# A build-time scheduler's three limits, constant before, now taken from a table by stretch of the run

## The chip, the cores and the metric

The kernel runs on one core of a Trainium2 chip. The metric is the device time of one execution in microseconds, median over several executions. "PE" in profile lines is TensorE's matmul, "PEld" its weight load, "DVE" is VectorE, "ACT" ScalarE, "POOL" GpSimd, "SP" the queue that issues most DMAs. All executions used here were in the fast state. One execution of each kernel was profiled; it can lie up to two microseconds from that kernel's median, so accounts inside an execution are made from profiles, and verdicts from medians and intervals.

## The reference, cut to what matters

A transformer block on 2048 tokens of width 512, with 32 heads of width 16 and a gated feed-forward part of width 1792.

```python
scores = jnp.einsum('bhqd,bhkd->bhqk', q, k) * Dh ** (-0.5)
p = _softmax(scores, axis=-1)
o = jnp.einsum('bhqk,bhkd->bhqd', p, v)
...                                   # output projection, residual, layer norm with modulation
return _gelu(x @ w_gate) * (x @ w_up) @ w_down
```

What costs is the exp: 32 x 2048 x 2048 scores, which the kernel handles as 2048 **blocks** of 128 x 512 scores of one head: 128 partitions, 512 columns.

## The kernel before

The program is written out by Python code that runs when the kernel is built. It keeps a time model of each engine, and at every step decides which instruction comes next. The chip then runs five fixed instruction streams. No scheduling happens on the chip.

ScalarE does most exps, three blocks in one instruction (a "triple") or two (a "pair"). VectorE takes some blocks by an integer trick, four at a time; these four are a **quad**. A quad also needs three shifted copies, each one instruction on VectorE or on GpSimd, and the values are then multiplied with all four copies.

```python
gb = self.scp[:, s0 + CH - 1, :]      # third bank of the group of three ...
if g is not None:                     # ... goes to VectorE when a quad is open
    ...
self.act(self.E[:, e0:e0 + n, :], self.scp[:, s0:s0 + n, :], ACT.Exp, scale=EXP_SCALE)
...
self.ts("dve", kq[:, 512 * j:512 * j + 512].bitcast(U16), gb, 128 / OCT, SHIFT_C, ALU.mult, ALU.add)
```

So an open quad turns ScalarE's triples into pairs. When a quad may open, and who does its shifts, depends on three limits:

```python
AHEAD = 20        # a round may become a quad only if it lies this many blocks ahead
PRESS = 5         # no exp to VectorE while a unit with so few plain rounds left lacks shifts
URGENT = 6        # a shift of a unit with so few plain rounds left goes first, and not to GpSimd
...
def urgency(self, tk):
    ...
    return 0 if self.plain[tk[1][1]] <= (URGENT if tk[1][1][3] == 512 else URG2) else 2
...
def pressed(self):
    return any(x.get("done", 0) < 3 and self.plain[x["rnd"][0]] <= (PRESS if x["rnd"][0][3] == 512 else PRE2) for x in self.wait)
```

A **unit** is one group of heads with one set of queries, a **round** is four blocks of a unit, and a quad is a round. The queries come in sets of 512, 512, 512, 256, 128 and 128 tokens, so attention has a long stage of 512-wide units and, from about 614 us, one of 256-wide units and then the last blocks. The feed-forward matmuls of a finished set are "side work", put into TensorE's gaps in the attention of the next sets. What is not done when attention ends is done in the **tail**, before the last 128 tokens can finish.

The time model gives a DMA a fixed time to land, which one of the experiments below changes:

```python
self.dma_free = max(t + 1400, self.dma_free) + cost / (350 if early else RATE)
op.t1 = self.dma_free + (1500 if early else LAND)          # LAND = 1300 ns
```

## Time and profile before

| | before |
|---|---|
| time, median of 4 | 807.35 us |
| profiled span | 805.0 us |
| ScalarE busy | 773.7 us (96%) |
| VectorE / TensorE / GpSimd busy | 83% / 93% / 34% |
| blocks on VectorE | 420 of 2048 (105 quads) |
| attention ends, tail | 778.0 us, then 27.0 us |

The table is read from top to bottom: ScalarE sets the time, VectorE's blocks relieve it, and the tail is what comes after the last exp of attention. The prediction shows the lines. Two lines that it uses without showing them are the groups by form of GpSimd's shifts in the kernel before (count, busy us, mean ns, then idle time before them and what ended it):

```profile
L393 POOL TENSOR_SCALAR mreg<-dreg 128x2048 uint16<-128x2048 uint16 x93 | 175.3, 1902 | 260.7 <-DVE mreg L393 105.7 <-PE ps_pv L368 41.2 <-DVE wreg L385 31.1
L393 POOL TENSOR_SCALAR mreg<-mreg 128x2048 uint16<-128x2048 uint16 x46 | 86.7, 1902 | 138.8 <-DVE mreg L393 47.1 <-DVE wreg L402 36.0 <-PE ps_pv L368 24.0
```

GpSimd does 93 + 46 = 139 of the 315 shifts.

### The profile page before, as it was taken

Reading aid. Unit: us, or ns where it says so; the run is one execution under the profiler, and the core shown is the slowest. Engines: PE = TensorE matmul, PEld = TensorE weight load, DVE = VectorE, ACT = ScalarE, POOL = GpSimd, SP = SyncE. Lnnn points to the kernel's source line nnn. Section 1 sums busy time; section 2 is a strip of 40 time slices with the busy share of each in tenths; the row PEclk is TensorE's granted clock in tenths of the full one; section 3 lists DMA queues with packets and bytes.
Section 4 is the critical chain, followed back from the end, with each engine's and each line's share of the span. In section 5 each row is a group of like instructions: output and inputs, shape, how many; then the busy total and the mean of one; then the engine's idle time right before and its main releaser. Section 6 shows DMA issues by size and latency. Waiting matters only on the chain.

```text
span 805.0 us, 27412 instructions
## 1 busy us (share of the span) xinstructions
PE 749.6 (93%) x12250; PEld 267.6 (33%) x12254; DVE 671.0 (83%) x1216; ACT 773.7 (96%) x728; POOL 277.7 (34%) x172
## 2 busy tenths in 40 slices
PE   8899999998899999999999899999999899999987
PEld 3333333322222222222222222222344342454455
DVE  7878898978898989988688998989778986677873
ACT  5999999999999999999999999999999999999982
POOL 3110335365546172456556346134262010000310
PEclk9999999999999999999999999999999999999999
DMA  9101000000022121111003111110123221120100
GB/s 310 58 9 19 10 10 16 10 16 10 16 55 68 35 55 36 48 41 29 24 27 108 36 52 51 48 42 17 42 59 89 63 75 37 34 75 14 23 9 14
DMA packets 58632, 36.03 MB, mean 45 GB/s; under 512 B 17977, under 2 KB 55090, under 8 KB 58514
## 3 DMA queue, kind: packets, MB, share of 16 engines
q1 hardware_dynamic: 56914, 32.84, 15.0%
q8 instruction: 96, 1.57, 0.8%
q10 hardware_dynamic: 1600, 1.44, 0.6%
q14 instruction: 22, 0.18, 0.1%
HBM read 29.62 MB, written 2.61 MB: 40 GB/s over the span
## 4 chain that ended last, share of the span: by engine, by line
ACT 89%; PE 8%; DVE 3%; issue 0%; DVEq 0%
ACT E L381 85%; PE ps_sc L368 4%; ACT wreg L381 3%; PE ps_mi L368 3%; PE ps_pv L368 1%; DVE mreg L393 1%; DVE kmo L402 0%; DVE xs L385 0%; DVE wreg L385 0%; PE ps_sc L372 0%; DVE hreg L393 0%; ACT L381 0%; DVE vaug L402 0%; DVE dreg L393 0%; DVE kme L393 0%
## 5 line engine op out<-in xcount | busy, mean ns | idle before, releaser
L381 ACT ACTIVATE E<-ps_sc 128x1024 bf16<-128x1024 f32 (+2 forms) x686 | 748.2, 1282 | 15.6 <-PE ps_sc L368 15.0
L393 POOL TENSOR_SCALAR mreg<-dreg 128x2048 uint16<-128x2048 uint16 x93 | 175.3, 1902 | 260.7 <-DVE mreg L393 105.7
L393 DVE TENSOR_SCALAR dreg<-ps_sc 128x512 uint16<-128x512 f32 x253 | 171.6, 685 | 34.3 <-PE ps_sc L368 31.8
L368 PE MATMUL ps_sc<-qT,kme 32*128 32x512 bf16 (+2 forms) x1313 | 168.3, 332 | 18.3 <-ACT E L381 15.1
L368 PE MATMUL ps_sc<-qT,kmo 32*128 32x512 bf16 (+2 forms) x1313 | 173.7, 332 | 9.7 <-ACT E L381 8.5
L368 PE MATMUL ps_pv<-E,vaug 128*17 128x512 bf16 (+2 forms) x2112 | 150.4, 327 | 0.8 <-DVE osb L402 0.5
L393 POOL TENSOR_SCALAR mreg<-mreg 128x2048 uint16<-128x2048 uint16 x46 | 86.7, 1902 | 138.8 <-DVE mreg L393 47.1
L368 PE MATMUL ps_pv<-mreg,vaug 128*17 128x512 bf16 (+2 forms) x1704 | 121.6, 337 | 1.7 <-DVE mreg L393 1.0
L393 DVE TENSOR_SCALAR mreg<-ps_sc 128x512 uint16<-128x512 f32 x126 | 85.4, 686 | 18.9 <-PE ps_sc L368 17.5
L368 PE MATMUL ps_mi<-wreg,mreg 128*32 128x512 bf16 (+1 forms) x1280 | 92.4, 372 | 4.4 <-DVE wreg L398 1.3
L368 PEld LDWEIGHTS ps_sc<-qT,kme 32*128 32x128 bf16 x1313 | 45.0, 91 | 143.7 <-ACT E L381 115.4
L368 PEld LDWEIGHTS ps_sc<-qT,kmo 32*128 32x128 bf16 x1313 | 45.7, 91 | 127.8 <-ACT E L381 109.3
L393 DVE TENSOR_SCALAR mreg<-dreg 128x2048 uint16<-128x2048 uint16 x117 | 76.8, 682 | 1.7 <-PE ps_pv L368 1.4
L368 PEld LDWEIGHTS ps_pv<-E,vaug 128*17 128x17 bf16 x2112 | 43.9, 89 | 61.5 <-issue 48.8
L368 PEld LDWEIGHTS ps_pv<-mreg,vaug 128*17 128x17 bf16 x1704 | 38.1, 89 | 36.8 <-issue 13.2
L402 DVE CAST wreg<-ps_mi 128x512 bf16<-128x512 f32 x49 | 33.5, 684 | 10.5 <-PE ps_mi L368 10.3
L368 PEld LDWEIGHTS ps_mi<-wreg,mreg 128*32 128x32 bf16 x1280 | 26.7, 95 | 44.0 <-issue 18.8
L368 PE MATMUL ps_mi<-hreg,wreg 128*32 128x512 bf16 x480 | 39.5, 385 | 0.0
L393 DVE TENSOR_SCALAR mreg<-mreg 128x2048 uint16<-128x2048 uint16 x59 | 38.4, 682 | 1.1 <-PE ps_pv L368 1.0
L398 DVE SCALAR_TENSOR_TENSOR wreg<-wreg,ps_mi 128x512 bf16<-128x512 bf16 x49 | 33.4, 682 | 6.5 <-PE ps_mi L368 5.1
L635 POOL TENSOR_SCALAR mv<-mv 128x4 f32<-128x4 f32 (+2 forms) x11 | 2.6, 239 | 94.5 <-DVE mv L425 93.9
L385 DVE TENSOR_TENSOR wreg<-wreg 128x1024 bf16<-128x1024 bf16 (+1 forms) x56 | 34.1, 616 | 0.5
(149 smaller groups left out, 670.8 us busy)
## 6 DMA issues: line engine op xcount, KB each, us to landing
mreg<-in_B_w_up_dram SPq DMA_DIRECT2D x22, 256.0 KB, 2.9
mreg<-in_B_w_gate_dram SPq DMA_DIRECT2D x15, 256.0 KB, 3.0
rb<-scr_rec SPq DMA_DIRECT2D x96, 32.0 KB, 1.8
dreg<-in_B_w_down_dram SPq DMA_DIRECT2D x9, 256.0 KB, 3.0
mreg<-in_w_mod_dram SPq DMA_DIRECT2D x1, 2048.0 KB, 13.3
mreg<-in_B_w_down_dram SPq DMA_DIRECT2D x8, 256.0 KB, 2.7
out_dram<-xs SPq DMA_DIRECT2D x16, 128.0 KB, 1.7
osb<-osb SPq DMA_DIRECT2D x48, 32.0 KB, 2.0
```

The source lines that it names most:

```text
L368: return self.rec("pe", lambda e: e.matmul(out, lhsT, rhs, start=start, stop=stop, tile_position=tp), [lhsT, rhs], [out], cost=(n, int(rhs ...
L381: return self.rec("act", lambda e: e.activation(out, in_, func, scale=scale, **kw), rd, wr, cost=self.cost("act", out, [in_], "act"))
L385: return self.rec(eng, lambda e: e.tensor_tensor(out, a, b, op), [a, b], [out], cost=self.cost(eng, out, [a, b], "tt"))
L393: return self.rec(eng, lambda e: e.tensor_scalar(out, a, s1, s2, **kw), rd, [out], cost=self.cost(eng, out, [a], "ts"))
L398: return self.rec("dve", lambda e: e.scalar_tensor_tensor(out, a, s, b, op0=op0, op1=op1), rd, [out], cost=self.cost("dve", out, [a, b], " ...
L402: return self.rec(eng, lambda e: e.tensor_copy(out, in_), [in_], [out], cost=self.cost(eng, out, [in_], "ts"))
L635: self.rec("pool", lambda e: e.tensor_scalar(v, v, EPS, None, op0=ALU.add), [v], [v], cost=200)
```

## The change

The intent is to open more quads by choosing the three limits for each sixteenth of the run. The table was picked offline: many were tried, and the one with the earliest end by the scheduler's own model was kept. An entry is (urgent, press, reach).

```diff
-AHEAD = 20
-PRESS = 5
-URGENT = 6
+PLAN = ((8, 6, 18), (9, 5, 16), (5, 5, 22), (5, 5, 22), (5, 5, 22), (5, 5, 22), (5, 5, 22), (5, 5, 22), (5, 5, 22), (9, 4, 18), (7, 6, 24), (5, 5, 22), (5, 5, 22), (5, 5, 22), (5, 5, 22), (7, 5, 24))
...
-        return 0 if self.plain[tk[1][1]] <= (URGENT if tk[1][1][3] == 512 else URG2) else 2
+        return 0 if self.plain[tk[1][1]] <= (self.limit[0] if tk[1][1][3] == 512 else URG2) else 2
...
+            self.limit = PLAN[min(len(PLAN) - 1, pos * len(PLAN) // nseq)]
...
-                    while quad is None and cand and rounds[cand[0]][2] < pos + (AHEAD1 if rounds[cand[0]][2] < nsplit else AHEAD):
+                    while quad is None and cand and rounds[cand[0]][2] < pos + (AHEAD1 if rounds[cand[0]][2] < nsplit else self.limit[2]):
```

The same is done to the limit in `pressed`.

> **What bounds the kernel now.** I read the engine totals of the page first, because they say which engine could be the limit. The kernel does attention for 32 heads and feeds the feed-forward part into its gaps.
>
> ```profile
> span 805.0 us, 27412 instructions
> ## 1 busy us (share of the span) xinstructions
> PE 749.6 (93%) x12250; PEld 267.6 (33%) x12254; DVE 671.0 (83%) x1216; ACT 773.7 (96%) x728; POOL 277.7 (34%) x172
> ...
> ## 4 chain that ended last, share of the span: by engine, by line
> ACT 89%; PE 8%; DVE 3%; issue 0%; DVEq 0%
> ```
>
> ScalarE is busy for 96% and carries 89% of the chain that ended last, nearly all of it the exp. TensorE's 93% is near enough to be a rival. Next I read the stretches view over stages: start, attention with 512-wide query blocks at full flow, its hand-over, the 256-wide blocks, the last blocks, the tail. Columns are length, then busy us and count of TensorE, its weight loads, VectorE, ScalarE, GpSimd.
>
> ```profile
> 13.00:116.00 103.00, 97.05 (x1795) 36.73 (x1799) 86.70 (x183) 100.58 (x95) 17.41 (x14) 1.00 0.15 46
> 116.00:570.00 454.00, 425.55 (x5685) 122.21 (x5679) 403.77 (x685) 453.44 (x434) 215.29 (x117) 1.00 0.14 38
> 570.00:614.00 44.00, 41.26 (x854) 16.77 (x850) 35.02 (x63) 44.00 (x42) 23.86 (x14) 1.00 0.30 80
> 614.00:728.00 114.00, 107.08 (x2173) 45.25 (x2166) 87.19 (x166) 114.00 (x97) 4.71 (x4) 1.00 0.20 52
> 728.00:778.00 50.00, 46.21 (x1361) 25.13 (x1353) 37.88 (x73) 49.85 (x46) 10.20 (x7) 1.00 0.08 18
> 778.00:805.00 27.00, 21.41 (x231) 16.31 (x235) 11.91 (x24) 8.35 (x16) 0.80 (x2) 0.96 0.03 11
> ```
>
> From 116 to 778 us ScalarE lacks 0.7 us of 662. So in the body the time **is** the sum of ScalarE's instructions; no wait is left there to remove. Last, the groups by form show what that sum is made of.
>
> ```profile
> L381 ACT ACTIVATE E<-ps_sc 128x1024 bf16<-128x1024 f32 x407 | 399.9, 1122 | 0.5 <-PE ps_sc L368 0.5
> L381 ACT ACTIVATE E<-ps_sc 128x1536 bf16<-128x1536 f32 x271 | 391.6, 1542 | 2.6 <-PE ps_sc L368 2.1
> ...
> L393 DVE TENSOR_SCALAR dreg<-ps_sc 128x512 uint16<-128x512 f32 x253 | 171.6, 685 | 34.3 <-PE ps_sc L368 31.8 <-DVE mreg L393 0.5 <-POOL mreg L393 0.3
> ...
> L393 DVE TENSOR_SCALAR mreg<-ps_sc 128x512 uint16<-128x512 f32 x126 | 85.4, 686 | 18.9 <-PE ps_sc L368 17.5 <-POOL mreg L393 0.5
> ```
>
> The scores are 2048 blocks of 512 columns. ScalarE takes 407 pairs and 271 triples (and one single): 814 + 813 + 1 = 1628. VectorE takes 253 + 126 from the score banks, and two smaller rows (27 and 14) from the spare bank: 420 blocks, or **105 quads** of four. 1628 + 420 = 2048, so the count closes.
>
> The durations overlap, so the means are not the price. The chain gives it:
>
> ```profile
> 723.86 4.03 ACT E L381 x3
> ...
> 739.34 27.60 ACT E L381 x25
> ```
>
> Three triples in 4.03 us are 1.343 us each. If 11 of the 25 are triples (14.77 us), the other 14 take 12.83 us, or 0.916 us a pair. One block therefore costs 1.343 - 0.916 = **0.427 us**. The check: 407 x 0.916 + 271 x 1.343 = 737 us, and with 28 tanh of the feed-forward part (21 at 0.934 and 7 at about 0.51 us, 23 us) 760 us, against 762 us from 16 to 778.
>
> **What the Trainium skill says.** "ScalarE: Activation LUTs", section "Step-by-step: what each stage is for", gives one element per cycle and lane, 0.833 ns an element, whatever the function. The trace agrees: 427 ns for 512 columns is 0.834 ns. "VectorE: DVE Perf Modes", section "The perf-mode tier table", gives a 16-bit tensor_scalar in SBUF a four-fold rate and none of it to an operand in PSUM with 32 bits. The trace agrees: 512 columns out of PSUM take 685 ns, a shift over 2048 columns in SBUF 682 ns. "SBUF — State Buffer", section "SBUF: two separate sides", says VectorE in its two-port modes and GpSimd exclude each other for a whole instruction. The trace is compatible: GpSimd's 139 shifts (93 + 46, 1902 ns each) stand idle longest behind VectorE's shifts, 105.7 us in the larger row. It doesn't prove the lock, as the kernel adds waits of its own there.
>
> **The change part by part.** It touches no instruction's form, buffer or amount of mathematics outside the split. A scheduler, run when the program is built, decides which rounds of four blocks become quads. Three limits that were constants (urgent 6, press 5, reach 20) now come from a table by sixteenth of the 2048 blocks; eleven of the sixteen hold (5, 5, 22).
>
> - *Urgent.* A quad needs three shifted copies. A shift is done early on VectorE, and barred from GpSimd, when its unit has no more than this many plain rounds left. 6 to 5 leaves shifts open to GpSimd a little longer. A shift moved there frees 0.68 us of VectorE and nothing on ScalarE.
> - *Press.* No exp goes to VectorE while a nearly finished unit still lacks shifts. 5 stays 5 in most entries; 4 and 6 each appear in places.
> - *Reach.* A round may become a quad only if it lies at least this many blocks ahead: 22 for 20, so it has a little more time, and late candidates are dropped sooner.
> - The limits on urgent and press bind only 512-wide units. The tail and the 256-wide stage are moved only by reach and by what comes before.
>
> One quad more moves four blocks: ScalarE saves 4 x 0.427 = **1.71 us**, all on the path (four triples become pairs, so the instruction count stays). VectorE pays 4 x 0.686 + 3 x 0.56 x 0.682 = 3.9 us (176 of 315 shifts run on it, 0.56), beside other work. TensorE multiplies the values with four sources rather than one: 3 x 4 sets of four matmuls; in the order of time four take 0.39 us and eight 0.61, so 0.215 a set and 2.6 us a quad, beside other work.
>
> What room is there? In 116 to 570 VectorE idles 454 - 403.8 = 50.2 us, enough for 13 quads. TensorE idles 28.5 us and plays 220 filler matmuls, 55 sets or 11.8 us, which it drops when it has work: 40 us, enough for 15. So 10 to 15 quads, 17 to 25 us, are an unreachable ceiling, as gaps are scattered and mostly under a microsecond (VectorE waits 31.8 us in all on scores, in 87 pieces in the largest row). These limits only choose among rounds and who shifts; I choose a fifth of that ceiling, **2.5 quads**, since the old constants were already tuned and a table by stretch, picked after trying many, should keep something. 2.5 x 1.71 = 4.3 us. I expect the offline choice to survive on the chip better than usual, because ScalarE never waits here, and its cost in the scheduler (0.833 ns a column plus 60 ns: 913 and 1340 ns) is within 0.4% of the 916 and 1343 measured.
>
> **Predicted: 807.3 - 4.3 = 803.0 us.**
>
> **Rivals.**
> 1. *Nothing comes of it.* The table fits the time model's noise; quads stay at 105 give or take one. For it: the change is tiny, and TensorE's releases on the chip may be later than modelled. Against it: ScalarE's waits on scores total 0.5 us in the body. Time 806 to 808.
> 2. *TensorE becomes the bound.* More quads bring 2.6 us each to an engine with 6% free, and ScalarE starts to wait for scores. For it: 93% busy, 17.5 and 31.8 us of VectorE's waits are on its scores. Against it: fillers give way first, and matmul busy time overstates. Each quad beyond about six would then bring less than it costs; 803 to 808.
> 3. *A large gain.* Shifts that move to GpSimd, idle for 239 of 454 us, free VectorE for five or more quads: 797 to 799. Against it: the GpSimd exclusion, and only two units of change in a limit.
> 4. *A jam at the end of a unit.* Later urgency leaves a unit's last shifts late, its accumulator bank is held, and TensorE and then ScalarE stall for a few us. The scheduler would see most of that. 808 to 812.
>
> **Range and chances.** Rival 1 sets the high end, 808; six quads set the low one, 807.3 - 10.2 = 797. A gain over 2%, to under 791.2 us, needs ten quads, the ceiling itself: 2%. A loss over 2% needs 16 us of new ScalarE idle time where there is now under 1: 1%.
>
> **What would show it.** The evictions in 512-column form should rise from 420 by about 10, to 430, and triples fall by as many as pairs rise. The time lost should be 0.427 us per block moved, within a microsecond. GpSimd's shifts should rise from 139 of 315, by 5 to 15. Pair and triple should cost the same 0.916 and 1.343. ScalarE should still lack under 1.5 us from 116 us to the tail. The tail, 27 us, should not change. The prediction is wrong if the block count stays and the time moves, which would make a wait, not the split, the cause; or if blocks move and the time doesn't follow, because ScalarE begins to wait.

## The result, and the profile after

The changed kernel took **802.36 us** (801.52 to 802.88, 4 runs) against 807.35 us (806.82 to 807.46, 4 runs). The ratio is 0.9939, with a 95% interval of 0.9921 to 0.9956. Ratios here are the mean time of one kernel's fast runs over that of the other's of the same rounds, so not quite the ratio of the medians quoted.

First the page of the changed kernel, for the lines shown of before:

```profile
span 801.0 us, 27439 instructions
## 1 busy us (share of the span) xinstructions
PE 746.0 (93%) x12243; PEld 268.8 (34%) x12247; DVE 690.8 (86%) x1254; ACT 765.8 (96%) x729; POOL 272.5 (34%) x169
...
ACT 78%; PE 10%; DVE 7%; DMA 2%; POOL 1%; issue 1%; SPq 1%; POOLq 0%; DVEq 0%
```

VectorE gained 19.8 us of work and ScalarE lost 7.9. The chain that ended last is less pure: ScalarE holds 78% of it, not 89%, and DMAs appear in it. Next the groups by form of the changed kernel, for the exps:

```profile
L379 ACT ACTIVATE E<-ps_sc 128x1024 bf16<-128x1024 f32 x432 | 424.6, 1111 | 1.5 <-PE ps_sc L366 1.5
L379 ACT ACTIVATE E<-ps_sc 128x1536 bf16<-128x1536 f32 x248 | 360.8, 1533 | 4.8 <-PE ps_sc L366 4.6
```

The pairs went from 407 to 432, the triples from 271 to 248. That is 864 + 744 = 1608 blocks on ScalarE, and **440 on VectorE, 110 quads, five more**. Between the end of one exp and the end of the next, the medians in the trace's records are 917 ns for a pair and 1343 ns for a triple in both kernels. With 25 pairs more and 23 triples fewer, the exp sum fell from 407 x 0.9165 + 271 x 1.343 + 0.5 (one single block) = 737.5 us to 432 x 0.9165 + 248 x 1.343 = 729.0 us, by 8.5 us or 20 x 0.427. The span fell by only 4.0. The stretches view of the changed kernel shows where ScalarE now idles (columns as in the prediction):

```profile
116.00:570.00 454.00, 424.69 (x5695) 122.13 (x5687) 410.97 (x694) 453.02 (x435) 215.28 (x117) 1.00 0.14 38
570.00:614.00 44.00, 41.08 (x878) 17.78 (x870) 38.89 (x74) 44.00 (x42) 23.79 (x14) 1.00 0.30 82
614.00:728.00 114.00, 108.18 (x2243) 46.22 (x2240) 96.35 (x179) 112.73 (x100) 6.61 (x5) 0.99 0.19 52
728.00:778.00 50.00, 45.90 (x1302) 27.33 (x1295) 37.48 (x77) 46.90 (x47) 6.49 (x5) 1.00 0.06 16
```

Until 614 us ScalarE is about as full as before. From 614 to 728 us it lacks 1.27 us where it lacked nothing, and up to 778 us 3.10 where it lacked 0.15 (a part of that is the tail, since attention now ends at 773.7). The waits view of ScalarE for 614 to 778 us is empty for the kernel before; for the changed one it holds one line (total us, times, longest):

```profile
ACT E L379 <- PE ps_sc L366: 4.3, 4, 1.5
```

Where did the five quads come from? The matmuls that multiply values with an exp show it by their width. Of those on a quad's four copies (one row for each of two buffers), the 512-wide ones are 1120 and 224 in **both** kernels (and 40 and 8 more that go to a score bank, again in both). The 256-wide ones, from the groups by form of the kernel before and then of the changed one:

```profile
L368 PE MATMUL ps_pv<-mreg,vaug 128*17 128x256 bf16 x376 | 16.7, 273 | 0.3 <-DVE mreg L393 0.2
...
L368 PE MATMUL ps_pv<-dreg,vaug 128*17 128x256 bf16 x72 | 3.5, 273 | 0.0
```

```profile
L366 PE MATMUL ps_pv<-mreg,vaug 128*17 128x256 bf16 x536 | 23.5, 273 | 0.1
...
L366 PE MATMUL ps_pv<-dreg,vaug 128*17 128x256 bf16 x104 | 5.1, 274 | 0.3 <-DVE osb L400 0.3
```

A 256-wide quad has 32 such matmuls, so there were 448 / 32 = 14 and are now 640 / 32 = 20. The 128-wide ones went from four quads to three. The net gain lies wholly in the narrower units, whose stage begins at about 614 us and in which two of the three limits do not act at all. Some of their exps are done before that stage begins. Counted by time, 36 + 313 + 30 + 21 + 20 blocks went to VectorE in the five stretches up to 116, 570, 614, 728 and the end, and 39 + 317 + 28 + 40 + 16 do now. It is mostly stretch 614 to 728 that gained.

An account of the two profiled executions, in microseconds (a wait is what an exp or tanh takes above its own price from the end of the one before it, for exps past 20 us):

| | before | after | difference |
|---|---|---|---|
| start to first exp | 13.5 | 14.0 | +0.5 |
| exp sum | 737.5 | 729.0 | -8.5 |
| tanh of the feed-forward part | 23.2 | 23.2 | 0 |
| ScalarE's waits | 3.4 | 7.0 | +3.6 |
| tail | 27.0 | 27.4 | +0.4 |
| sum (the span is 805.0 and 801.0) | 804.6 | 800.6 | -4.0 |

So two questions are open after the result. Does the number of quads set the time? And what are the new waits?

### The profile page after: what moved, and what is told of

Same layout as the page of the kernel before. It is cut to its first block, busy times and chain, and to the rows that moved or that the text cites. A ratio compares the mean times of both kernels' runs of the same rounds, so it can differ in the third digit from the quotient of the medians.

```text
span 801.0 us, 27439 instructions
## 1 busy us (share of the span) xinstructions
PE 746.0 (93%) x12243; PEld 268.8 (34%) x12247; DVE 690.8 (86%) x1254; ACT 765.8 (96%) x729; POOL 272.5 (34%) x169
## 4 chain that ended last, share of the span: by engine, by line
ACT 78%; PE 10%; DVE 7%; DMA 2%; POOL 1%; issue 1%; SPq 1%; POOLq 0%; DVEq 0%
ACT E L379 75%; PE ps_sc L366 4%; PE ps_mi L366 3%; ACT wreg L379 3%; PE ps_pv L366 2%; DVE mreg L391 2%; DVE dreg L391 1%; DMA den<-scr_den 1%; POOL mreg L391 1%; SPq L430 1%; DVE wreg L396 0%; DMA rb<-scr_rec 0%; DVE wreg L383 0%; DVE xs L383 0%; DMA scr_rec<-rden 0%
## 5 line engine op out<-in xcount | busy, mean ns | idle before, releaser
L391 POOL TENSOR_SCALAR mreg<-dreg 128x2048 uint16<-128x2048 uint16 x98 | 184.4, 1897 | 315.5 <-DVE mreg L391 84.0
L391 DVE TENSOR_SCALAR dreg<-ps_sc 128x512 uint16<-128x512 f32 x267 | 181.5, 686 | 38.8 <-PE ps_sc L366 36.7
L366 PE MATMUL ps_sc<-qT,kme 32*128 32x512 bf16 (+2 forms) x1319 | 174.0, 332 | 14.0 <-ACT E L379 11.2
L366 PE MATMUL ps_pv<-mreg,vaug 128*17 128x512 bf16 (+2 forms) x1816 | 128.1, 335 | 1.8 <-DVE mreg L391 0.7
L391 POOL TENSOR_SCALAR mreg<-mreg 128x2048 uint16<-128x2048 uint16 x38 | 71.8, 1898 | 94.8 <-DVE mreg L391 62.1
L391 DVE TENSOR_SCALAR mreg<-ps_sc 128x512 uint16<-128x512 f32 x137 | 92.5, 684 | 11.2 <-PE ps_sc L366 10.6
L391 DVE TENSOR_SCALAR mreg<-dreg 128x2048 uint16<-128x2048 uint16 x121 | 80.8, 688 | 0.4
L391 DVE TENSOR_SCALAR mreg<-mreg 128x2048 uint16<-128x2048 uint16 x73 | 48.8, 690 | 0.6 <-PE ps_pv L366 0.5
L379 ACT ACTIVATE wreg<-wreg 128x1024 bf16<-128x1024 bf16 (+1 forms) x28 | 29.5, 1053 | 0.0
```

The costliest lines, as they stand in the source:

```text
L366: return self.rec("pe", lambda e: e.matmul(out, lhsT, rhs, start=start, stop=stop, tile_position=tp), [lhsT, rhs], [out], cost=(n, int(rhs ...
L379: return self.rec("act", lambda e: e.activation(out, in_, func, scale=scale, **kw), rd, wr, cost=self.cost("act", out, [in_], "act"))
L391: return self.rec(eng, lambda e: e.tensor_scalar(out, a, s1, s2, **kw), rd, [out], cost=self.cost(eng, out, [a], "ts"))
```

## The experiments

**Theory A**: the time is the exp sum, 0.427 us for each block on VectorE, plus a fixed rest. **Theory B**: the exp sum is only half of it; how attention ends and hands over to the tail decides what of the saving arrives. **Theory C**, on the new waits: they have causes that the scheduler's model does not contain, namely a clock dip and a DMA round trip.

Before any run, I ran the build step alone on many variants and counted what they give to VectorE. That costs no chip time and settles some points, because equal programs need no timing. These counts are of the build and not of a run on the chip; entries are counted from 0. Setting the last four table entries back to (6, 5, 20) gives the same instructions of the same shapes on the same tiles, in the same order, on all five engines. Three quads are then the neighbouring round of their unit, so that 168 TensorE matmuls read another part of the same tiles, and the modelled end does not move. So those four entries do next to nothing, although the extra quads lie there: the gain there follows from the state that earlier stretches leave. Entries 2 to 5, set back one at a time, change no block count either. And if reach is 20 everywhere but 22 in entry 11, the changed kernel's block counts come back in every sixteenth. So, counted in blocks, that one number separates the changed kernel from the first run below. The scheduler's own model ends the changed kernel at 795.5 us and that first run at 802.2.

### 1. Same number of quads, and fewer, in other arrangements

Four tables, each replacing `PLAN` in the changed kernel:

```diff
# limits_only: the table's first two limits, reach 20 everywhere
-PLAN = ((8, 6, 18), (9, 5, 16), (5, 5, 22), ...
+PLAN = ((8, 6, 20), (9, 5, 20), (5, 5, 20), ...
# uni_5_5_22: the commonest entry everywhere
+PLAN = ((5, 5, 22),) * 16
# uni_5_5_24
+PLAN = ((5, 5, 24),) * 16
# last4_reach22
+PLAN = ((6, 5, 20),) * 12 + ((6, 5, 22),) * 4
```

> The table's first two limits alone, reach 20 everywhere. The built program again gives 440 blocks (110 quads) to VectorE, as the changed kernel does. Theory A (the number of blocks sets the time, 0.427 us each, and the new waits stay those of the changed kernel): about 802.4 us, within 0.5 of the changed kernel. Theory B (the same exp sum, but the end of attention and its hand-over to the tail decide what of it arrives): the schedule leaves ScalarE idle some 6 us longer before the tail, so 806 to 810 us. Unit of evidence: exp sum as in the changed kernel (432 pairs, 248 triples) and the time from the last exp of attention to the end, 27 us or longer by 5 to 8.

> The table's commonest entry (5, 5, 22) in all sixteen places: is the table by stretch needed? The program gives 428 blocks to VectorE, 8 more than before. Theory A: 807.3 - 8 x 0.427 = 803.9 us. Theory B: 804 to 808 us, the exp sum 3.4 us shorter and part of it lost in waits at the end.

> (5, 5, 24) in all sixteen places: the program gives 440 blocks to VectorE, as many as the changed kernel. Theory A: 798.8 us, or 802.4 with the changed kernel's waits. Theory B: the saving is lost at the end of attention, where the schedule has gaps of 6 and 8 us: 807 to 812 us, no faster than before in spite of 20 more blocks.

> The old limits in the first twelve sixteenths, only the reach 22 in the last four: 432 blocks on VectorE, 12 more than before, all in the last three sixteenths. Theory A: 807.3 - 12 x 0.427 = 802.2 us. Theory B: blocks added so near the end delay the last feed-forward work and the hand-over, 809 to 814 us, slower than before.

Measured, with the kernel before at 807.58 us in the same rounds. The last three columns are of the profiled execution.

| run | blocks on VectorE | median us | ratio to before (95%) | exp sum | attention ends | tail |
|---|---|---|---|---|---|---|
| before | 420 | 807.58 | | 737.5 | 778.0 | 27.0 |
| limits_only | 440 | 808.04 | 1.0008 (0.9995 to 1.0021) | 729.0 | 770.9 | 35.3 |
| uni_5_5_22 | 428 | 805.39 | 0.9973 (0.9959 to 0.9986) | 734.0 | 773.9 | 28.3 |
| uni_5_5_24 | 440 | 811.92 | 1.0048 (1.0034 to 1.0063) | 729.0 | 772.8 | 36.9 |
| last4_reach22 | 432 | 812.05 | 1.0054 (1.0042 to 1.0066) | 732.3 | 773.3 | 36.2 |

Theory A falls. limits_only and uni_5_5_24 give VectorE as many blocks as the changed kernel and have its exp sum, but they are 5.7 and 9.6 us slower than its 802.36; last4_reach22 has 12 blocks more than before and is slower than before. The saving did arrive at the end of attention: all four reach it 4 to 7 us earlier than the kernel before. Three of them give it back in the tail, which takes 35 to 37 us instead of 27.

What fills that tail? The stretches view from the end of attention to the end, for uni_5_5_24, and its rows of TensorE in that stretch that belong to the down projection in the bank for side work:

```profile
772.80:809.70 36.90, 29.08 (x251) 18.36 (x249) 15.97 (x34) 8.38 (x17) 1.60 (x4) 0.98 0.05 15
```

```profile
L366 PE MATMUL ps_mi<-xs,hreg 128*128 128x512 bf16 x24 | 6.5, 381 | 2.8 <-DVE wreg L383 1.8 <-DVE xs L383 0.5 <-DVE hreg L396 0.5
L366 PE MATMUL ps_mi<-dreg,hreg 128*128 128x512 bf16 x16 | 4.6, 379 | 0.0
```

The tail itself needs 14 such matmuls, one tile of 128 tokens; the kernel before has 7 + 6 records of them there (a record can be missing). Here there are 40: two more tiles, left over from the set before, 11.1 us of busy time in place of 3.6. TensorE works 29.1 us in the tail instead of 21.4. limits_only (36 such matmuls in rows of these two kinds) and last4_reach22 (39) show the same; uni_5_5_22, which gives little back, has 13. So work was left over when attention ended: shorter exps had shortened the very time into which the feed-forward work has to fit. The scheduler's model has part of this. It ends uni_5_5_24 at 804.8 and last4_reach22 at 807.9 us, behind the changed kernel's 795.5.

### 2. Fewer quads at the end

The next two runs forbid new quads in the last part, and leave the program as it is until then.

```diff
-                    elif (cand and self.quad_free and ...
+                    elif (cand and pos < 1960 and self.quad_free and ...     # on uni_5_5_24
+                    elif (cand and pos < 1920 and self.quad_free and ...     # on the changed kernel
```

> (5, 5, 24) everywhere, but no new quad once 1960 of the 2048 blocks are passed: the program differs only at the end and gives 428 blocks to VectorE instead of 440, three quads fewer. If blocks alone set the time, 12 x 0.427 = 5.1 us slower than the run with (5, 5, 24), about 817 us. If the late quads' extra TensorE work (2.6 us each) pushed feed-forward matmuls past the end of attention, those come back under it: 40 down-projection matmuls after the last exp fall to about 13, the tail from 36.9 to 27 to 29 us, and the time to 803 to 807 us, faster with fewer quads.

> The changed kernel, but no new quad past 1920 of 2048 blocks: the same program until then, 424 blocks on VectorE, four quads fewer. What is a quad worth where nothing spills? If 1.71 us, 802.4 + 6.8 = 809.2 us with the tail still at 27 us. If TensorE is what limits the changed kernel's end too, the quads bought little there: 802.5 to 806 us, with the waits of ScalarE after 600 us (3.7 us) shrinking.

The first of these carries over from the prediction a wrong price, 2.6 us of TensorE time for a quad; it is 0.65, as shown further down.

| run | blocks on VectorE | median us | ratio to before (95%) | attention ends | tail |
|---|---|---|---|---|---|
| uni_5_5_24 | 440 | 811.92 | 1.0048 | 772.8 | 36.9 |
| u5524_no_quad_past_1960 | 428 | 806.89 | 0.9986 (0.9968 to 1.0004) | 776.3 | 27.0 |
| the changed kernel | 440 | 802.36 | 0.9939 | 773.7 | 27.4 |
| after_no_quad_past_1920 | 424 | 808.12 | 0.9996 (0.9983 to 1.0009) | 779.3 | 27.0 |

Three quads fewer made uni_5_5_24 five microseconds **faster**. The tail of that run, in the same two views as above:

```profile
776.30:803.30 27.00, 21.62 (x236) 16.31 (x236) 11.91 (x24) 8.36 (x17) 0.80 (x2) 0.99 0.03 11
```

```profile
L366 PE MATMUL ps_mi<-xs,hreg 128*128 128x512 bf16 x8 | 2.1, 379 | 0.0
L366 PE MATMUL ps_mi<-dreg,hreg 128*128 128x512 bf16 x6 | 1.8, 379 | 0.0
```

The leftover is gone: 14 matmuls, and 27.0 us. That the late quads had crowded it out is shown; on which engine they did so is not. The stretches view from 750 us to the end of attention, for uni_5_5_24 and then for the run without late quads:

```profile
750.00:772.80 22.80, 20.53 (x784) 13.36 (x777) 18.86 (x38) 22.76 (x21) 9.42 (x5) 1.00 0.06 14
750.00:776.30 26.30, 24.09 (x718) 12.87 (x706) 11.34 (x25) 26.23 (x21) 0.81 (x2) 1.00 0.07 20
```

TensorE is about as full in both (90% and 92%), while VectorE, for which leftover matmuls in the tail of uni_5_5_24 waited 2.8 us (the line shown), falls from 83% to 43%. (The kernel before, which leaves nothing over, had 91% and 76% there.) So VectorE's load is a rival to TensorE's, and no run parts the two.

In the changed kernel, where nothing is left over, four quads fewer cost 5.8 us (808.1, near the 809.2 expected of a full price). The exp sum rose by 6.9 us (to 735.9), and 1.2 us of waits went. A quad is thus worth 1.7 us of exp sum, and it arrives only while the side work still fits. Theory B stands.

### 3. The new waits: a DMA round trip

At 769.5 us the changed kernel's ScalarE waits 1.5 us. The chain of waits leads back from there to DMAs: the denominators go to memory, are read back in another layout, inverted, written and read again (three hops of 2.95, 3.04 and 3.63 us in the chain). VectorE's order of time in the changed kernel shows what hangs on the last hop:

```profile
762.58 0.96 DVE L403 RECIPROCAL rb<-ps_mi 128x128 f32<-128x128 f32 x1
766.32 0.42 DVE L383 TENSOR_TENSOR onorm<-osb,rb 128x256 bf16<-128x256 f32 x1 [2.78 <-DMA rb<-scr_rec]
766.66 0.28 DVE L383 TENSOR_TENSOR onormp<-osb,rb 128x128 bf16<-128x128 f32 x1
766.87 0.95 DVE L403 RECIPROCAL rb<-ps_mi 128x128 f32<-128x128 f32 x1
```

VectorE stands 2.78 us at a normalisation whose operand has not landed. Behind it, in order, waits a reciprocal whose input is there; on this reciprocal hangs the next product, on that TensorE's output projection, and behind that projection stand the scores that ScalarE needs. The model let the normalisation go first, because it took the DMA for faster. The edit makes the model's DMAs later from 750 us on:

```diff
-            op.t1 = self.dma_free + (1500 if early else LAND)
+            op.t1 = self.dma_free + (1500 if early else LAND + (800 if t > 750000 else 0))
```

> The changed kernel, but from 750 us of modelled time on the scheduler counts 0.8 us more for each DMA to land; the same 440 blocks, the same program before. If the ScalarE wait of 1.6 us at 769.5 us comes from a denominator round trip that the model took for shorter than it is, the new order doesn't put a waiting normalisation ahead on VectorE and that wait goes: 800.8 to 801.8 us. If it has another cause it stays: 802.4 us or, by the scheduler's own choice, 0.8 us more.

It took **800.64 us** (800.55 to 801.0), ratio 0.9912 (0.9899 to 0.9924), just below the range expected of the order on VectorE. Compared instruction by instruction, the built program differs from the changed kernel by **one VectorE instruction, moved by two places**; the other four engines have the same streams:

```
 Reciprocal rb<-ps_mi 128x128
-TensorTensor onorm<-osb,rb 128x256
 TensorTensor onormp<-osb,rb 128x128
 Reciprocal rb<-ps_mi 128x128
+TensorTensor onorm<-osb,rb 128x256
```

To make sure, I ran the changed kernel once more beside two versions, with 0.4 us (the instruction moves by one place only, still ahead of the reciprocal) and with 0.8 us again.

> The changed kernel once more, on the same chip as the next two: 801.5 to 803 us, with the ScalarE wait of about 1.6 us near 769 us and the clock dip near 670 us in the trace if they belong to the program and not to one execution.

> As the run with 0.8 us more for each DMA from 750 us on, with 0.4 us. The built program differs from the changed kernel in one VectorE instruction moved by one place: the waiting normalisation stands behind the small product, but still ahead of the reciprocal that TensorE's output projection needs. If that reciprocal behind the DMA is the cause, the wait stays, and so do 801.5 to 803 us; if any later place helps, 800.6 to 801.5.

> The run with 0.8 us once more; against the changed kernel it moves that one VectorE instruction by two places, behind the reciprocal, and nothing else. 800.3 to 801.2 us, 1.3 to 1.9 under the changed kernel of this call; if the first result was chance, the same as it.

| run | median us | range, executions | ratio to before (95%) | wait near 768 us, profiled |
|---|---|---|---|---|
| after_again (the changed kernel) | 801.96 | 799.72 to 803.9, 6 | 0.9929 (0.9913 to 0.9945) | 0.36 |
| late_dma_400 (one place) | 802.67 | 802.55 to 803.39, 5 | 0.9941 (0.9928 to 0.9954) | 1.54 |
| late_dma_again (two places) | 800.87 | 800.76 to 801.21, 4 | 0.9916 (0.9904 to 0.9929) | 0.26 |

The same stretch of VectorE in late_dma_again:

```profile
764.10 0.96 DVE L403 RECIPROCAL rb<-ps_mi 128x128 f32<-128x128 f32 x1 [0.60 <-PE ps_mi L366]
764.98 0.36 DVE L383 TENSOR_TENSOR onorm<-osb,rb 128x256 bf16<-128x256 f32 x1
```

The reciprocal goes 2.8 us earlier, and the normalisation finds its data landed. One place did not help, two did, as expected of the reciprocal. The size is about 1.8 us against late_dma_400 and 1.1 to 1.7 against the changed kernel (1.1 in the last call, less than the 1.3 to 1.9 expected). The changed kernel itself spreads over 4 us, and its interval in the last call overlaps that of late_dma_again. Its profiled execution there was a quick one of 800.69 us, in which the wait was only 0.36 us. So the wait is not in every execution of the changed kernel. Part of the spread goes with the clock: in after_again the two executions with a mean clock of 1.000 took 799.72 and 800.69 us, the four with 0.996 to 0.998 took 801.70 to 803.90. With executions at 0.996 to 0.998 alone, the changed kernel's eight of both calls took 801.52 to 803.90 us, and seven with the instruction moved took 800.55 to 801.21. So the gain holds at like clocks.

### 4. The new waits: a clock dip

At 674.3 us the changed kernel's ScalarE waits 1.35 us. No engine is late by its own waits there: TensorE is slow. The stretches view of the changed kernel around it; the column after POOL is the granted clock:

```profile
666.00:670.00 4.00, 2.85 (x72) 1.17 (x68) 3.61 (x7) 4.00 (x4) 0.00 (x0) 1.00 0.07 21
670.00:674.00 4.00, 3.48 (x42) 1.00 (x41) 1.68 (x4) 3.05 (x3) 1.90 (x1) 0.65 0.04 11
```

TensorE is busy 2.85 of 4 us, and in the next 4 us it is granted 0.65 of its clock: the same busy time holds 42 matmuls in place of 72. The scheduler plays filler matmuls against this, by a count of columns in the last 3.4 us. The edit raises that count for this place:

```diff
-        return FILL - w
+        return FILL + (600 if 655000 < t < 680000 else 0) - w
```

> The changed kernel, but between 655 and 680 us of modelled time the scheduler asks for 600 columns more of matmul in each stretch of 3.4 us before it is content, so more fillers are played. In the changed kernel the granted clock fell to 0.65 at 670 to 674 us after TensorE had idled, and ScalarE waited 1.35 us there. If too little TensorE work caused it, the clock stays at 1.0 in that window and the wait goes. The schedule after it differs and has one quad less (436 blocks, +1.7 us): 802.4 - 1.35 + 1.7 = 802.8, 801.5 to 804.5 us. If the dip is chance it shows up here or there regardless.

```profile
666.00:670.00 4.00, 3.36 (x84) 1.39 (x72) 3.61 (x7) 4.00 (x4) 0.00 (x0) 1.00 0.14 21
670.00:674.00 4.00, 3.49 (x65) 1.34 (x68) 3.05 (x6) 4.00 (x5) 1.90 (x1) 1.00 0.03 8
```

These are the same stretches of after_fill. The clock stays at 1.00 and ScalarE is full (4.00). The time is 802.42 us (801.45 to 803.0), ratio 0.9932 (0.992 to 0.9945). That is no gain. The new order has one quad fewer (436 blocks), and by the prices above the 1.35 us saved pay for its 1.7.

One execution without a dip proves little, since the one profiled in after_again had none either, with the changed kernel's own program. Cuts at whole microseconds hide why. In every profiled execution here the records of the clock begin and end on edges 3.41 us apart, and these edges fall at another place of the program in each execution. The stretches view cut at these edges, for the changed kernel (the stretch before the dip, and the dip), then for the same place in after_again and in after_fill:

```profile
667.76:671.17 3.41, 1.75 (x38) 0.57 (x34) 3.41 (x8) 3.41 (x4) 1.11 (x1) 1.00 0.06 17
671.17:674.59 3.42, 3.42 (x46) 1.02 (x38) 1.10 (x3) 2.18 (x3) 0.79 (x1) 0.50 0.07 17
668.68:672.09 3.41, 1.99 (x38) 0.69 (x42) 3.14 (x6) 3.41 (x5) 1.64 (x1) 1.00 0.04 11
669.04:672.45 3.41, 2.66 (x50) 0.91 (x50) 2.67 (x6) 3.41 (x5) 1.79 (x1) 1.00 0.04 10
```

Before the dip TensorE was busy 1.75 us of such a stretch. The four other profiled executions with a dip here (after_no_quad_past_1920, after_late_dma, late_dma_400 and late_dma_again) had 1.74 to 1.76 us. In after_again the edges fell half a microsecond later in the same program, and the stretch held 1.99 us. In after_fill no 3.41 us between 664 and 672 us hold less than 2.26, wherever they are cut. So the edit did remove the thin place, and what looked like chance is, at least in part, where the edges fall. This was read from the traces after the runs, one execution each. No rule of busy time follows: in the tails of uni_5_5_22 and late_dma_again stretches with 1.73 and 1.75 us were followed by no dip. And three of the five executions of after_fill have a mean clock of 0.997, so dips may have come elsewhere.

### 5. A version that beats both

The experiments say what a better table has to respect: a later DMA, and no quads at the very end. I searched again offline with both, starting from the changed kernel's table.

```diff
-LAND = 1300
+LAND = 1700
-PLAN = ((8, 6, 18), (9, 5, 16), (5, 5, 22), (5, 5, 22), ...
+PLAN = ((8, 6, 18), (9, 5, 16), (5, 6, 20), (5, 4, 24), (7, 5, 22), (6, 5, 20), (5, 5, 22), (5, 5, 22), (5, 5, 22), (5, 5, 22), (8, 5, 16), (7, 4, 22), (7, 4, 22), (5, 5, 16), (5, 5, 16), (5, 5, 16))
-                    elif (cand and self.quad_free and ...
+                    elif (cand and pos < 2000 and self.quad_free and ...
```

> An attempt at a better version: the scheduler counts 1.7 us instead of 1.3 for a DMA to land in the whole run, no new quad past 2000 blocks, and a new table chosen offline under that. The program gives 440 blocks to VectorE, as the changed kernel does, so the exp sum is the same 729 us. If the later DMA assumption keeps waiting work out of VectorE's way and nothing spills into the tail (13 to 16 down-projection matmuls after attention, tail 27 to 28 us), 799 to 801.5 us, under the changed kernel's 802.2. If a new table is worth no more than its model, and spills on the chip, 803 to 808 us.

It took **798.65 us** (798.11 to 798.98, 4 executions) against 807.12, ratio 0.9891 (0.9875 to 0.9908). The block count and the exp sum are the changed kernel's (440 and 729.1 us); what differs is the waits, 2.3 us in all and 0.3 after 600 us, where the changed kernel had 7.0 and 3.7. The stretches view of its late attention:

```profile
614.00:728.00 114.00, 109.34 (x2260) 47.58 (x2256) 95.63 (x179) 114.00 (x102) 6.60 (x5) 1.00 0.20 53
728.00:770.00 42.00, 39.31 (x1194) 22.83 (x1190) 31.70 (x65) 41.98 (x39) 2.70 (x3) 1.00 0.07 15
```

ScalarE lacks 0.02 us of 156, the clock stays at 1.00 (its mean is 0.999 or 1.000 in all four executions), and the tail is 27.4 us with 13 down-projection records. The time is just below the 799 us expected at best. Three things were altered at once, so which of them did it is not separated.

## Why the prediction was right or wrong

- **The time came out, 803.0 against 802.36 us, and the bound was read rightly.** ScalarE's body is a sum of exps, and the prices of 0.916 and 1.343 us for a pair and a triple held to a nanosecond. That a block is worth 0.427 us of exp sum held as well (8.5 us for 20), and so did VectorE's cost: its busy time rose by 19.8 us for five quads, 3.96 each against 3.9 predicted.
- **The term "2.5 quads" was mis-sized by two.** It was "a fifth of that ceiling", a choice. Five came, and the exp sum fell by 8.5 us, not 4.3. The step "since the old constants were already tuned" undervalued a search over many tables.
- **"The time lost should be 0.427 us per block moved, within a microsecond" failed.** Of 8.5 us, 4.0 arrived in the profiled execution and 5.0 in the medians; 3.6 went into waits after 600 us that did not exist before. From 116 us to the end of attention ScalarE lacked 4.1 us, not under 1.5, so the prediction's own last sign of being wrong came half true. This error and the one above offset each other, so it is luck that the time came out. The runs named two of these waits, the one-instruction order on VectorE behind a DMA (up to 1.6 us) and the clock dip (1.35 us).
- **The room was looked for in the wrong stage.** The prediction counted VectorE's idle time from 116 to 570 us. There the number of 512-wide quads did not change at all (the matmul counts are equal), and all the net gain lies in the narrower units of the stage after 614 us. VectorE had 26.8 us free there (114 - 87.2), which the shown stretches already held.
- **"Shifts open to GpSimd a little longer" failed.** Its shifts were to rise from 139 by 5 to 15 and fell to 136; VectorE's rose from 176 to 194. The quads came without that help.
- **"The tail and the 256-wide stage are moved only by reach and by what comes before" was half right.** Reach in the last four entries changes neither a count nor the modelled end; what comes before does the rest. The tail, 27.4 us, stayed as predicted.
- **TensorE's price of 2.6 us a quad was wrong by four.** I took four sets of matmuls for each source. A 512-wide round has one key tile, so a source is one set of four, and a quad adds 3 x 0.215 = 0.65 us. The counts confirm it: 100 filler matmuls went (408 to 308), the quads brought 6 x 24 - 48 = 96, and TensorE's instructions stayed at 12250 and 12243. Rival 2 was thus described wrongly: up to 600 us ScalarE waited no more than before (7.0 - 3.7 = 3.3 us, against 3.4 in the whole kernel before), and two of the later waits on scores were traced to other causes. What showed elsewhere was side work left for the tail in three other tables, a way that no rival named.
- **"I expect the offline choice to survive on the chip better than usual" was too hopeful.** By its own model the table gained 8.6 us (804.1 to 795.5 us), the whole exp saving; on the chip 5.0 of it arrived. The model was right about ScalarE and wrong about landing times and the clock.

## What to carry to other kernels

When one engine is full and the price of its instructions is known, work moved off it can be valued to a few tenths of a microsecond by counting, but only up to the end of that stage. Then ask what else had to fit into the time that has now become shorter, and look whether it turns up behind. With programs that a search arranges, count before you time: streams of the same instructions need no run, and one in-order instruction that stands ahead of others while it waits for a DMA can cost one to two microseconds, here as much as a quad is worth.

## What the Trainium skill lacked or had wrong

- "TensorE: Matmul & The Clock Gate", table in "What's actually happening", lets the clock fall after at least one idle window of about 3.4 us. Here the granted clock fell to 0.50 for 3.41 us after a stretch of 3.41 us in which TensorE was still busy for 1.75, and stayed at 1.00 after 1.99 and 2.66. Too little work was enough, without a wholly idle window. No page gives the share of work that is enough.
- "DMA: Bandwidth & Descriptors", section "Anatomy of one DMA — SWDGE (gpsimd) path", fits about 2.0 us of fixed time to a small transfer of another path. The profile's medians for 4 and 8 KB transfers issued from SP were 1.5 to 2.1 us, but the three hops on the chain that mattered took 2.95, 3.04 and 3.63 us (the last is of a larger kind, with medians of 1.7 and 1.8, and counts from the last of four issues in a row). No page gives the spread of the whole time of such transfers.
- No page says what it costs when an in-order vector queue holds a ready instruction behind one that waits for a DMA. Here it was up to 1.6 us of ScalarE time, nearly all removed by moving one instruction by two places (0.26 us left).
